# Batch 0's second product: two of four plain row tiles go over to seven half products, and the side work around them is put in another order

## The chip, the cores and the metric

The kernel runs on one core of a Trainium2 chip. The metric is the device time of one execution in microseconds. A profile of one execution comes with it: every instruction of the five engines (PE for matrix products, with its weight loads as PEld; DVE, ACT and POOL for elementwise work; SP for issuing transfers) with its start, its duration and what it waited for. "L362" is line 362 of the kernel.

## The reference, cut to what matters

A block-sparse attention (4 batches, 8 heads, 768 rows, head size 64) feeds a two-layer network with a gated activation.

```python
k_sum = k.reshape(B, H, nb, block, D).max(axis=3)      # blocks of 32 rows
v_sum = v.reshape(B, H, nb, block, D).mean(axis=3)
scores = concat(local window of 16 of q @ k.T, q @ k_sum.T + log(block))
x = softmax(scores) @ concat(v, v_sum)                 # 3072 x 512
h = x @ w_in                                           # 512 -> 2048
g = h * sigmoid(beta * h)
out = g @ w_out                                        # 2048 -> 512
```

The kernel takes `silu(beta * h)` on ACT and multiplies `w_out` by `1 / beta` once, in place, in 16 slices of 128 x 512 (`scale_w_out`, L361).

## The kernel before, in words

**Batches.** A batch is 768 rows. For each one the attention gives `xT`, the first product gives `h_sb` (16 tiles of 128 columns of the hidden layer, all 768 rows), and the second product gives six row tiles (`ms` 0 to 5) of 128 x 512 outputs. While PE does the two products of one batch, the attention of the next one is done as side work.

**Two ways through the second product.** A plain row tile is 16 matmuls of 512 columns, in four atoms of four (`o_atom`, L714; matmul at L706); ACT copies the result out and SP stores it. The other way takes two row tiles `t` and `t + 3` together by Winograd's form of Strassen's scheme: the inner dimension, the rows and the columns are halved, and seven products of 8 matmuls of 256 columns (`product`, L752; matmul at L755) take the place of eight. It needs three sums of pieces of `h_sb` in `s_sb` and one in place (`h_sums`, L738), three sums of pieces of `w_out` in `t_sb` and one in place (`w_sums`, L746), and additions of the seven results (`gather`, L764): two copies `p`, a copy of the lower half, the sums `u2` and `u3`, and three last additions. The products are issued in the order 1, 6, 5, 4, 2, 7, 3. Batch 0 uses the plain way for row tiles 0, 3, 4 and 1 and the seven products for the pair (2, 5); later batches use the seven products throughout.

**Order.** `run` (L828) issues a list of main steps, all of them PE work with its results. Every piece of side work has a number in `AT`; after main step `i` all pieces with a number below `i + 1` are issued, by rising number. So the whole part of a number is the main step behind which a piece stands in the queue of its engine, and each engine works through its queue in order. `ENG` names the engine of a piece: `d` is DVE, `a` is ACT, `p` is POOL (GpSimd).

```python
main.extend([lambda p=p: h_two(p, 2) for p in range(k2 // 2)])                      # steps 0-7
main.extend([lambda i=i: h_half(i, 1, HB[i % 3][:, 0]) for i in range(k2)])         # 8-23
main.extend([lambda ms=ms, a=a: o_atom(0, ms, a) for ms in (0, 3, 4, 1) for a in range(4)])   # 24-39
products(0, (2,))                                                                   # 40-46
```

**Side work of this stretch.** `kt` transposes batch 1's keys on PE (`kt_pe`, L418) and copies windows of them into `kw` (`windows_perm`, L369, two copies a group); `km` takes the block maxima on DVE (L382) and copies them into `kw` (`key_sums`, L389); `scale` does four slices of `w_out` each; `qt` does the queries; `vl1` issues the loads of batch 1's values on POOL (`cast_v`, L250) and `vo1` shifted copies of them on SP (L489); `exp1` loads ACT's exponential table (L825); `sc1` is the scores on PE with the exponential on ACT (L456, L470), `mk1` the mask on DVE (L474); `vm1` the block means (L505); `sp1` their spreading (L515); `av1` the weighting with its division (L526, L560); `xd1` the transposes to `xT` by transfers from ACT's queue (L572). Scores of even halves use the PSUM pair `big2`, those of odd halves `big1`: a second score into a pair waits until ACT has taken the exponential of the first. A product of the first layer in steps 8 to 23 goes to one of three banks in turn (`HB`) and is freed by ACT's activation.

Of the kernel before, what the change touches and what calls it, by code (L numbers as in the profile page):

```python
# [33 lines left out]
    'xd1': [37.4, 39.05, 41.0, 41.5],
    'kl2': [31.49, 27.509, 31.14, 31.359],
    'ql2': [44.528, 45.846, 48.477, 49.061],
    'vl2': [48.656, 50.666, 53.32, 55.633],
    'kd2': [47.896, 48.564, 50.287, 53.981],
    'win2': [48.822, 54.925, 59.06, 64.294],
    'kx2': [50.116, 57.618, 60.611, 66.447],  # L40
    'ks2': [57.494, 58.64, 61.796, 70.807],
    'qd2': [53.645, 55.686, 56.34, 64.339],
# [12 lines left out]
    'kd3': [83.91, 86.33, 85.635, 89.794],
    'win3': [91.341, 93.68, 91.196, 100.991],
    'kx3': [93.659, 96.229, 96.044, 103.349],
    'ks3': [93.765, 97.224, 99.448, 104.103],
    'qd3': [91.148, 91.216, 90.659, 93.011],
    'vo3': [97.047, 94.075, 98.896, 104.362],  # L60
    'exp3': [99.362],
    'sc3': [101.902, 101.912, 104.132, 104.349, 106.423, 106.507, 108.144, 108.507],
    'mk3': [101.907, 104.547, 106.019, 106.041, 107.656, 107.74, 109.6, 109.7],
    'silu3': [120.261],
    'vm3': [106.738],
# [8 lines left out]
ENG = {  # L74
    'kw1': 'dddd', 'qt1': 'ddaa', 'x0': 'dd', 'ks1': 'pppp', 'scale': 'd' * 16, 'oc': 'aaaa',
    'vm1': 'dada', 'vm2': 'dada', 'vm3': 'dada', 'sp1': 'ddd', 'sp2': 'daa', 'sp3': 'daa',
    
    'win2': 'dddd', 'win3': 'dddd', 'ks2': 'pppp', 'ks3': 'pppp',
    'mk1': 'd' * 8, 'mk2': 'd' * 8, 'mk3': 'd' * 8,
    'g02': 'aaap', 'g10': 'aaap', 'g11': 'aaap', 'g12': 'aaap', 'g20': 'aaap', 'g21': 'aaap', 'g22': 'aaap',  # L80
    'g30': 'aaap', 'g31': 'aaap', 'g32': 'aaap',
}
# [68 lines left out]
def kernel(  # L151
# [576 lines left out]
    def late_tiles():
        p = opened("late")
        scope["half"] = p  # L730
        s_sb = p.tile([P, 3, J2, HS], bf16, name="s_sb")
        OPERANDS.update({1: (A11, B11), 2: (A12, B21), 3: (s_sb[:, 2], B22), 4: (A22, t_sb[:, 2]),
                         5: (s_sb[:, 0], t_sb[:, 0]), 6: (s_sb[:, 1], t_sb[:, 1]), 7: (A21, B12)})

    def tt(eng, o, a, b, op):
        eng.tensor_tensor(out=o, in0=a, in1=b, op=op)  # L736
# [297 lines left out]
```

## Time and profile before

| | |
|---|---|
| median of 3 runs | 207.76 us (207.07 to 209.65) |
| the profiled execution | 207.91 us, its span 206.2 us |
| TensorE's granted clock | 1.00 throughout |
| PE busy | 198.1 us (96% of the span) |
| DVE busy | 139.0 us (67%) |
| ACT busy | 126.8 us (61%) |
| POOL busy | 79.4 us (38%) |

The span runs from the first to the last instruction; 1.7 us of the execution's time lie outside it. Busy time of PE counts pipelined matmuls as one stretch. Rows of the chain of waits give a start, a length, an engine, the tile written, a line and a count; rows of the timeline give start, length, engine, line, operation, tiles, shapes and, in brackets, idle time before it and its cause. Rows of a table by stretches give the stretch, its length, and then for PE, PEld, DVE, ACT and POOL the busy time with the number of instructions.

### The profile page before, as it was taken

Reading aid. Unit: us, or ns where it says so; the run is one execution under the profiler, and the core shown is the slowest. Engines: PE = TensorE matmul, PEld = TensorE weight load, DVE = VectorE, ACT = ScalarE, POOL = GpSimd, SP = SyncE. Lnnn points to the kernel's source line nnn. Section 1 sums busy time; section 2 is a strip of 40 time slices with the busy share of each in tenths; the row PEclk is TensorE's granted clock in tenths of the full one; section 3 lists DMA queues with packets and bytes.
Section 4 is the critical chain, followed back from the end, with each engine's and each line's share of the span. In section 5 each row is a group of like instructions: output and inputs, shape, how many; then the busy total and the mean of one; then the engine's idle time right before and its main releaser. Section 6 shows DMA issues by size and latency. Waiting matters only on the chain.

```text
span 206.2 us, 5853 instructions
## 1 busy us (share of the span) xinstructions
PE 198.1 (96%) x2420; PEld 139.5 (68%) x2424; DVE 139.0 (67%) x327; ACT 126.8 (61%) x197; POOL 79.4 (38%) x112
## 2 busy tenths in 40 slices
PE   7799999999999999999999999999999999999993
PEld 2577766665555775666887866657888866568882
DVE  4567555799979950779799522589789475797132
ACT  2279686588787116767986139668895457792210
POOL 7976992402970049600093379601201100000011
PEclk9999999999999999999999999999999999999999
DMA  6999999999996849999799999999524620000222
GB/s 115 186 172 196 207 206 203 206 193 156 141 180 78 205 98 157 147 137 150 127 185 116 181 153 195 155 156 167 116 105 110 151 103 0 0 3 0 102 101 105
DMA packets 86794, 28.17 MB, mean 137 GB/s; under 512 B 75232, under 2 KB 83824, under 8 KB 86768
## 3 DMA queue, kind: packets, MB, share of 16 engines
q0 software_dynamic: 57632, 13.67, 73.4%
q1 hardware_dynamic: 19360, 11.63, 26.4%
q10 hardware_dynamic: 9776, 2.50, 7.1%
q8 instruction: 19, 0.31, 0.6%
q14 instruction: 7, 0.06, 0.1%
HBM read 27.73 MB, written 6.29 MB: 165 GB/s over the span
## 4 chain that ended last, share of the span: by engine, by line
PE 83%; DMA 7%; DVE 4%; issue 3%; POOL 2%; POOLq 0%
PE big L674 21%; PE one L755 15%; PE acc L755 10%; PE one L706 7%; PE one L674 5%; PE big L602 5%; DMA xT<-xn 4%; PE one L608 4%; DMA qrow<-in_q_dram 3%; PE big L462 3%; PE big L647 2%; PE big L415 2%; PE big L534 2%; PE big L608 2%; PE big L449 1%
## 5 line engine op out<-in xcount | busy, mean ns | idle before, releaser
L674 PEld LDWEIGHTS <-w_in_sb 128*128 128x128 bf16 x352 | 34.4, 98 | 22.9 <-issue 0.5
L674 PE MATMUL big<-xT,w_in_sb 128*128 128x384 bf16 x280 | 47.5, 326 | 0.3 <-DMA xT<-xn 0.3
L664 ACT ACTIVATE h_sb<-big,beta_sb 128x768 bf16<-128x768 f32 x39 | 34.6, 901 | 20.2 <-PE big L674 18.7
L736 POOL TENSOR_TENSOR o_sb<-p,u 128x256 f32<-128x256 f32 x10 | 7.3, 725 | 79.8 <-DVE u L736 59.9
L755 PEld LDWEIGHTS <-h_sb 128*128 128x128 bf16 x320 | 30.6, 98 | 4.5 <-issue 0.2
L755 PE MATMUL one<-w_out_sb,h_sb 128*128 128x256 bf16 x240 | 30.2, 273 | 0.2 <-ACT o_sb L393 0.2
L470 ACT ACTIVATE e<-big,bias 128x768 bf16<-128x768 f32 x32 | 27.3, 900 | 4.1 <-PE big L462 2.2
L755 PEld LDWEIGHTS <-s_sb 128*128 128x128 bf16 x240 | 23.2, 98 | 2.8
L736 DVE TENSOR_TENSOR u<-one,p 128x256 f32<-128x256 f32 x20 | 8.4, 422 | 18.1 <-PE one L755 18.0
L399 POOL COPY kw<-km 128x288 bf16<-128x288 bf16 x12 | 7.1, 596 | 34.2 <-DVE km L386 23.0
L253 POOL DMA_DIRECT2D ve<-in_v_dram x15 | 17.1, 1172 | 4.3 <-PE one L929 3.2
L706 PE MATMUL one<-w_out_sb,h_sb 128*128 128x512 bf16 x61 | 14.5, 380 | 0.4 <-issue 0.3
L474 DVE TENSOR_TENSOR e<-e,mask 128x768 bf16<-128x768 bf16 x24 | 12.9, 563 | 1.8 <-ACT e L470 1.6
L674 PE MATMUL one<-xT,w_in_sb 128*128 128x384 bf16 x72 | 14.0, 326 | 0.0
L393 ACT COPY o_sb<-one 128x256 f32<-128x256 f32 (+1 forms) x14 | 6.0, 432 | 12.6 <-PE one L755 7.8
L736 DVE TENSOR_TENSOR s_sb<-h_sb 128x768 bf16<-128x768 bf16 (+2 forms) x15 | 7.6, 508 | 9.2 <-ACT h_sb L682 7.1
L592 POOL DMA_DIRECT2D qn<-in_q_dram x16 | 13.4, 872 | 0.0
L592 POOL DMA_DIRECT2D kn<-in_k_dram x16 | 13.3, 856 | 0.0
L561 DVE TENSOR_TENSOR xn<-big,r 128x768 bf16<-128x768 f32 x12 | 11.5, 958 | 0.4
L386 DVE TENSOR_REDUCE km<-kT 128x24 bf16<-128x768 bf16 x12 | 11.2, 945 | 0.7 <-ACT kT L393 0.6
L602 PE MATMUL big<-xT,w_in_sb 128*128 128x384 bf16 x64 | 11.4, 326 | 0.0
L755 PE MATMUL acc<-t_sb,h_sb 128*128 128x256 bf16 x80 | 10.9, 273 | 0.0
(156 smaller groups left out, 339.7 us busy)
## 6 DMA issues: line engine op xcount, KB each, us to landing
out_dram<-o_sb SPq DMA_DIRECT2D x23, 256.0 KB, 3.2
ve<-in_v_dram POOLq DMA_DIRECT2D x14, 208.0 KB, 12.7
w_in_sb<-in_moe_w_in_dram POOLq DMA_DIRECT2D x4, 512.0 KB, 9.5
w_out_sb<-in_moe_w_out_dram POOLq DMA_DIRECT2D x4, 512.0 KB, 13.6
kn<-in_k_dram POOLq DMA_DIRECT2D x16, 96.0 KB, 4.7
qn<-in_q_dram POOLq DMA_DIRECT2D x16, 96.0 KB, 5.8
vo<-ve SPq DMA_DIRECT2D x12, 107.2 KB, 3.6
qrow<-in_q_dram POOLq DMA_DIRECT2D x4, 192.0 KB, 6.0
```

Of the source, the lines that this page charges most:

```text
L253: nc.gpsimd.dma_start(out=ve[:, g, 0:n, 0:D], in_=bass.AP(src.tensor, src.offset - W * D, [[D, P], [P * D, n], [1, D]]))
L470: nc.scalar.activation(out=e[:], in_=s[:, :, 0:HS], func=ACTF.Exp, bias=bias[:, 0:1], scale=scale)
L474: eng_of(ENG[f"mk{b}"][2 * g + u]).tensor_mul(out=e.rearrange("p h (m q) -> p h m q", q=QT), in0=e.rearrange("p h (m q) -> p h m q", q=QT) ...
L561: nc.vector.tensor_mul(out=x[:, 3 * us[0]:3 * us[0] + 3 * n].rearrange("p (k j) h d -> p k (j h) d", k=n), in0=tv[:, :, :, 0:D], in1=r[:, ...
L592: nc.gpsimd.dma_start(out=t[:, :, h], in_=pair(k if nm == "k" else q, b, g)[h].rearrange("(j p) d -> p j d", p=P))
L602: nc.tensor.matmul(t[:, 0:HS], w_in_sb[:, ki, i * P:(i + 1) * P], xT[:, ki, 0:HS], start=(ki == 0), stop=(ki == k1 - 1))
L608: nc.tensor.matmul(t[:, 0:HS], w_in_sb[:, ki, i * P:(i + 1) * P], xT[:, ki, lo:lo + HS], start=(ki == 0), stop=(ki == k1 - 1))
L664: nc.scalar.activation(out=h_sb[:, i, :].rearrange("p (k m) -> p k m", k=2), in_=t[:, :, 0:HS], func=ACTF.Silu, scale=beta_sb[:, i:i + 1])
L674: nc.tensor.matmul(o, w_in_sb[:, ki, i * P:(i + 1) * P], x, start=(ki == 0), stop=(ki == k1 - 1))
L706: nc.tensor.matmul(t[:, 0:hi - lo], h_sb[:, n, ms * P:(ms + 1) * P], w_out_sb[:, n, lo:hi], start=(n == 0), stop=(n == k2 - 1))
L736: eng.tensor_tensor(out=o, in0=a, in1=b, op=op)
L755: nc.tensor.matmul(SLOTS[n], a[:, j, t * P:(t + 1) * P], b[:, j], start=(j == 0 and n not in (2, 3, 7)), stop=(j == J2 - 1), skip_group_ch ...
```

## The change

Batch 0 now does row tiles 0 and 3 the plain way and the pairs (1, 4) and (2, 5) by seven products each. Main steps 24 to 31 are plain atoms, 32 to 38 the products of the new pair, 39 to 45 those of the old one; batch 1 begins with step 46 in place of 47.

- The sums of `h_sb` cover 256 columns a half in place of 128, and are cut in two along the inner dimension: eight operations of 128 x 1024 elements in place of four.
- `s_sb` moves out of the memory that is opened when the first inputs are done with (`late`) and is there from the start.
- Of the 16 slices of `w_out`, seven are scaled on POOL; slices 4 to 7 come first, behind step 8.
- One of the four window copies (group 2), the first of the two late `x0` copies and one query copy (group 0) go to ACT, two of four copies of maxima to DVE, all four copies of the means to DVE, one spreading copy to ACT (in batch 3 one comes back to DVE), and the last pair's second `p` copy to DVE. (Of the queries, group 1 stays on DVE.)
- The exponential's table is loaded behind step 27 in place of 23; the scores, masks, means and weighting of batch 1 stand otherwise around the products.
- For batches 2 and 3 most numbers fall by one with the main steps. Batch 2's loads, transposes, window copies and maxima also change places among themselves. With the numbers as they are, batch 2's copies of the block maxima of head pairs 2 and 3 stand ahead of the reductions that make them (58.389 ahead of 58.488, 61.875 ahead of 61.978), and that of pair 1 behind the scores that read it (71.221 behind 66.132 and 66.349): these three pairs use the block maxima that batch 1 left.

```diff
-    'scale': [8.3, 16.158, 16.833, 21.634],
+    'scale': [14.35, 8.574, 20.331, 22.721],
-    'km': [13.223, 16.831, 22.5, 23.85],
+    'km': [11.879, 13.674, 23.619, 20.213],
-    'ws': [24.0, 25.6, 26.6, 40.5],
-    'hs0': [36.284, 36.98, 42.604, 40.783],
-    'vl1': [5.1, 5.2, 5.3, 5.4],
-    'vo1': [23.54, 24.1, 25.1, 26.1],
-    'exp1': [23.6],
-    'sc1': [27.05, 27.06, 29.05, 29.06, 31.06, 31.07, 34.05, 34.06],
-    'mk1': [27.6, 27.7, 29.7, 29.8, 31.7, 32.2, 34.7, 34.8],
+    'ws': [23.767, 23.768, 24.034, 31.733],
+    'hs0': [22.405, 26.401, 26.413, 31.452, 26.412, 27.813, 30.612, 28.413],
+    'vl1': [8.158, 7.14, 5.008, 9.785],
+    'vo1': [26.807, 25.496, 27.73, 30.17],
+    'exp1': [27.302],
+    'sc1': [27.303, 27.729, 29.212, 31.973, 31.223, 30.064, 34.796, 34.969],
+    'mk1': [29.459, 30.059, 33.831, 33.913, 33.713, 33.906, 35.361, 36.679],
-    'vm1': [31.05],
-    'sp1': [31.2, 32.3, 32.31],
-    'av1': [36.5, 36.6, 39.5, 39.6],
+    'vm1': [28.088],
+    'sp1': [31.732, 36.0, 33.907],
+    'av1': [36.162, 36.678, 39.375, 39.789],
...
-    'kw1': 'dddd', 'qt1': 'ddaa', 'x0': 'dd', 'ks1': 'pppp', 'scale': 'd' * 16, 'oc': 'aaaa',
-    'vm1': 'dada', 'vm2': 'dada', 'vm3': 'dada', 'sp1': 'ddd', 'sp2': 'daa', 'sp3': 'daa',
+    'kw1': 'ddad', 'qt1': 'adaa', 'x0': 'ad', 'ks1': 'pddp', 'scale': 'dppdppdpddpddpdd', 'oc': 'aaaa', 'vm1':
+    'dddd', 'vm2': 'dada', 'vm3': 'dada', 'sp1': 'dad', 'sp2': 'daa', 'sp3': 'dda', 'win2': 'dddd', 'win3':
...
+    'dddd', 'ks2': 'pppp', 'ks3': 'pppp', 'mk1': 'dddddddd', 'mk2': 'dddddddd', 'mk3': 'dddddddd', 'g01':
+    'aaap', 'g02': 'adap', 'g10': 'aaap', 'g11': 'aaap', 'g12': 'aaap', 'g20': 'aaap', 'g21': 'aaap', 'g22':
...
+    s_sb = const.tile([P, 3, J2, HS], bf16, name="s_sb")
...
-        s_sb = p.tile([P, 3, J2, HS], bf16, name="s_sb")
...
-    main.extend([lambda ms=ms, a=a: o_atom(0, ms, a) for ms in (0, 3, 4, 1) for a in range(4)])
-    products(0, (2,))
+    main.extend([lambda ms=ms, a=a: o_atom(0, ms, a) for ms in (0, 3) for a in range(4)])
+    products(0, (1, 2))
...
-    at("hs0", [lambda i=i: h_sums(0, J2, 2 * P, (i,)) for i in range(4)])
+    at("hs0", [lambda i=i, h=h: h_sums(4 * h, 4 * h + 4, P, (i,)) for h in range(2) for i in range(4)])
```

More of the change, by code (lines that the diff above doesn't have):

```diff
@@ L15 @@
     'av0': [1.99, 4.754],
-    'x0': [5.759, 6.564],
-    'scale': [8.3, 16.158, 16.833, 21.634],
-    'clear': [6.428, 6.644],
-    'kt': [7.9, 9.6],
-    'km': [13.223, 16.831, 22.5, 23.85],
-    'qt': [25.5, 25.51],
-    'late': [32.254],
-    'ws': [24.0, 25.6, 26.6, 40.5],
-    'hs0': [36.284, 36.98, 42.604, 40.783],
-    'vl1': [5.1, 5.2, 5.3, 5.4],
-    'vo1': [23.54, 24.1, 25.1, 26.1],
-    'exp1': [23.6],
-    'sc1': [27.05, 27.06, 29.05, 29.06, 31.06, 31.07, 34.05, 34.06],
-    'mk1': [27.6, 27.7, 29.7, 29.8, 31.7, 32.2, 34.7, 34.8],
@@ L30 @@
-    'silu1': [34.957],
-    'vm1': [31.05],
-    'sp1': [31.2, 32.3, 32.31],
-    'av1': [36.5, 36.6, 39.5, 39.6],
[L34 to L42, printed above, removed]
@@ L55 @@
[L55 to L65, printed above, removed]
@@ L66 @@
-    'sp3': [107.773, 109.1, 110.3],
-    'av3': [110.1, 110.251, 113.15, 113.759],
-    'xd3': [110.535, 112.753, 114.844, 117.713],
+    'x0': [6.99, 6.995],
+    'scale': [14.35, 8.574, 20.331, 22.721],
+    'clear': [6.271, 5.688],
+    'kt': [7.573, 9.8],
+    'km': [11.879, 13.674, 23.619, 20.213],
+    'qt': [25.303, 25.489],
+    'late': [27.157],
+    'ws': [23.767, 23.768, 24.034, 31.733],
+    'hs0': [22.405, 26.401, 26.413, 31.452, 26.412, 27.813, 30.612, 28.413],
+    'vl1': [8.158, 7.14, 5.008, 9.785],
@@ new lines @@
+    'vo1': [26.807, 25.496, 27.73, 30.17],
+    'exp1': [27.302],
+    'sc1': [27.303, 27.729, 29.212, 31.973, 31.223, 30.064, 34.796, 34.969],
+    'mk1': [29.459, 30.059, 33.831, 33.913, 33.713, 33.906, 35.361, 36.679],
+    'silu1': [45.987],
+    'vm1': [28.088],
+    'sp1': [31.732, 36.0, 33.907],
+    'av1': [36.162, 36.678, 39.375, 39.789],
+    'xd1': [36.881, 37.347, 40.707, 41.901],
+    'kl2': [29.131, 27.069, 33.83, 32.89],
+    'ql2': [45.198, 45.471, 45.197, 48.451],
+    'vl2': [44.93, 52.008, 49.933, 49.966],
@@ new lines @@
+    'kd2': [46.896, 52.012, 49.287, 53.919],
+    'win2': [59.938, 56.775, 52.159, 65.497],
+    'kx2': [48.237, 51.576, 58.488, 61.978],
+    'ks2': [62.273, 71.221, 58.389, 61.875],
+    'qd2': [53.739, 52.151, 60.104, 61.874],
+    'vo2': [62.96, 63.625, 63.901, 65.498],
+    'exp2': [61.633],
+    'sc2': [63.902, 63.912, 66.132, 66.349, 68.423, 68.507, 70.144, 70.507],
+    'mk2': [64.2, 66.547, 68.019, 68.041, 69.656, 69.74, 71.6, 71.7],
+    'silu2': [82.261],
+    'vm2': [68.738],
+    'sp2': [69.773, 71.1, 72.3],
@@ new lines @@
+    'av2': [72.1, 72.251, 75.15, 75.759],
+    'xd2': [72.535, 74.753, 76.844, 79.713],
+    'kl3': [75.5, 74.5, 72.5, 73.5],
+    'ql3': [84.72, 82.832, 82.154, 84.128],
+    'vl3': [86.046, 85.957, 90.359, 91.448],
+    'kd3': [82.91, 85.33, 84.635, 88.794],
+    'win3': [90.341, 92.68, 90.196, 99.991],
+    'kx3': [92.659, 95.229, 95.044, 102.349],
+    'ks3': [92.765, 96.224, 98.448, 103.103],
+    'qd3': [90.148, 90.216, 89.659, 92.011],
+    'vo3': [96.047, 93.075, 97.896, 103.362],
+    'exp3': [98.362],
@@ L69 @@
+    'sc3': [100.902, 100.912, 103.132, 103.349, 105.423, 105.507, 107.144, 107.507],
+    'mk3': [100.907, 103.547, 105.019, 105.041, 106.656, 106.74, 108.6, 108.7],
+    'silu3': [119.261],
+    'vm3': [105.738],
+    'sp3': [106.773, 108.1, 109.3],
+    'av3': [109.1, 109.251, 112.15, 112.759],
+    'xd3': [109.535, 111.753, 113.844, 116.713],
     'xq1': [-0.443, -0.159, -0.972, -0.722],
@@ L74 @@
 ENG = {
-    'kw1': 'dddd', 'qt1': 'ddaa', 'x0': 'dd', 'ks1': 'pppp', 'scale': 'd' * 16, 'oc': 'aaaa',
-    'vm1': 'dada', 'vm2': 'dada', 'vm3': 'dada', 'sp1': 'ddd', 'sp2': 'daa', 'sp3': 'daa',
[L78 to L81, printed above, removed]
[4 rows of a table added]
+    'aaap', 'g30': 'aaap', 'g31': 'aaap', 'g32': 'aaap',
 }
@@ L726 @@
     t_sb = const.tile([P, 3, J2, DH], bf16, name="t_sb")
+    s_sb = const.tile([P, 3, J2, HS], bf16, name="s_sb")
+    OPERANDS.update({1: (A11, B11), 2: (A12, B21), 3: (s_sb[:, 2], B22), 4: (A22, t_sb[:, 2]),
+                     5: (s_sb[:, 0], t_sb[:, 0]), 6: (s_sb[:, 1], t_sb[:, 1]), 7: (A21, B12)})
     def late_tiles():
@@ L730, in late_tiles @@
         scope["half"] = p
-        s_sb = p.tile([P, 3, J2, HS], bf16, name="s_sb")
-        OPERANDS.update({1: (A11, B11), 2: (A12, B21), 3: (s_sb[:, 2], B22), 4: (A22, t_sb[:, 2]),
-                         5: (s_sb[:, 0], t_sb[:, 0]), 6: (s_sb[:, 1], t_sb[:, 1]), 7: (A21, B12)})
     def tt(eng, o, a, b, op):
```

11 lines of the change are left out of this document (removed).

## The prediction, on record before the result

> **What bounds the kernel now.** First the page's head: which engine has no room.
>
> ```profile
> span 206.2 us, 5853 instructions
> ## 1 busy us (share of the span) xinstructions
> PE 198.1 (96%) x2420; PEld 139.5 (68%) x2424; DVE 139.0 (67%) x327; ACT 126.8 (61%) x197; POOL 79.4 (38%) x112
> ```
>
> PE stands still for 8.1 us of the whole span. Then the table by stretches, for the stage that is changed and the ones ahead of it and behind.
>
> ```profile
> 36.70:48.93 12.23, 12.21 (x129) 7.59 (x129) 11.32 (x26) 9.75 (x17) 2.53 (x5) 1.00 1.62 190
> 48.93:69.00 20.07, 19.70 (x345) 10.78 (x347) 18.04 (x33) 14.46 (x21) 9.95 (x12) 1.00 1.30 145
> ```
> ```profile
> 75.20:122.90 47.70, 46.86 (x535) 33.90 (x533) 30.47 (x64) 30.12 (x44) 23.52 (x29) 1.00 1.45 147
> ```
>
> From 36.70 to 69.00 PE is busy 31.91 of 32.30 us, so the stage is worth what PE's instructions are worth; but DVE is busy 29.36 of these, 91%. That is the second limit: the change must not make PE wait for it. Third, the chain of waits through the stage, start and length.
>
> ```profile
> 48.93 1.89 PE one L706 x8
> 50.81 1.48 PE big L415 x64
> ...
> 54.13 0.46 PE big L462 x24
> ...
> 58.71 0.51 PE big L509 x28
> ...
> 62.37 0.46 PE big L462 x24
> ...
> 64.66 0.88 PE big L534 x48
> ...
> 69.11 1.85 PE one L755 x16
> 70.97 1.75 PE acc L755 x16
> ```
>
> It is PE from end to end. The eight scores stand in four rows, of which the first and the last are shown: 0.46/2 = 0.23 us each. The four weightings stand in two rows alike, 0.44 us each.
>
> **PE's work.** From 48.93 to 69.11 are 20.18 us. Queries (1.48), eight scores (4 x 0.46), means (0.51) and four weightings (2 x 0.88) take 5.59 of it, which leaves 14.59 us for the 64 plain matmuls: 0.228 each (some records of them are missing, so I divide by the 64 of the code). A half product's matmul takes 1.75/16 = 0.109 us by the last row. The change removes 32 x 0.228 = 7.30 us and adds 56 x 0.109 = 6.10: **-1.2 us**. Scores, weightings and transposes only change places on PE. The end behind the products carries this on: the first product of batch 1 starts when PE gets there, if nothing else is late.
>
> **ACT.** Here the order of the table load costs something.
>
> ```profile
> 49.55 1.28 ACT L826 ACT_TABLE_LOAD   x1
> ...
> 54.16 0.58 ACT L393 COPY o_sb<-one 128x512 f32<-128x512 f32 x1 [0.33 <-PE one L706]
> 54.65 1.70 ACT L470 ACTIVATE e<-big,bias 128x768 bf16<-128x768 f32 x2
> ```
>
> The load ran while ACT had nothing to do. Now it stands behind step 27 and so behind the copy of row tile 0, which ends at 54.74: load to 56.02, the exponentials from about 56.1, 0.85 apart, the first done at 57.0. The third score (group 1's first half) writes the same pair of banks; PE reaches it behind six atoms (6 x 0.912), the queries, two scores and the means, at 48.93 + 5.47 + 1.48 + 0.46 + 0.51 = 56.85. With the hand-over PE waits 0.2 to 0.4; a second wait of 0.1 falls on group 1's other half, two scores later. I take **+0.4**.
>
> ACT's further pieces lie beside PE: group 2's window copy (about 1.3 us by DVE's row below, with ACT's 0.58 for a copy of 512 columns and twice 1.3 as bounds) comes in the stretch 36.70 to 48.93, where ACT has 2.48 us free, and delays activations by less than the two steps that the three banks allow; if not, 0.1 to 0.3 us. The `x0` copy ends a step ahead of its use.
>
> **DVE, the walk.** These rows give the prices; where rows follow each other I use the distance.
>
> ```profile
> 37.61 2.69 DVE L396 COPY kw<-big 128x960 bf16<-128x960 bf16 x4 [1.21 <-PE big L415]
> ...
> 46.80 2.34 DVE L362 TENSOR_SCALAR w_out_sb<-w_out_sb,inv_beta 128x512 bf16<-128x512 bf16 x8
> 49.07 1.80 DVE L382 TENSOR_REDUCE km<-kw 128x24 bf16<-128x768 bf16 x2
> 50.79 1.21 DVE L736 TENSOR_TENSOR t_sb<-w_out_sb 128x2048 bf16<-128x2048 bf16 x1
> 51.92 1.80 DVE L396 COPY qn<-big 128x768 bf16<-128x768 bf16 x2
> 53.66 2.47 DVE L736 TENSOR_TENSOR t_sb<-w_out_sb,t_sb 128x2048 bf16<-128x2048 bf16 x2
> 56.04 1.02 DVE L474 TENSOR_TENSOR e<-e,mask 128x768 bf16<-128x768 bf16 x2
> ...
> 60.19 0.70 DVE L396 COPY vo<-vm_sb 32x768 bf16<-32x768 bf16 x2
> ...
> 72.20 0.68 DVE L736 TENSOR_TENSOR h_sb<-h_sb 128x1024 bf16<-128x1024 bf16 x1
> 72.80 0.42 DVE L736 TENSOR_TENSOR u<-one,p 128x256 f32<-128x256 f32 x1
> ```
>
> Prices: a group's windows 1.33, a slice's scaling 0.29, a reduction 0.88, a sum of `w_out` 1.17, a query copy 0.90, a mask 0.51, a spreading copy 0.35 (four make 1.4), a sum of `h_sb` 0.60, `u` 0.4. A means copy moves a sixth of a spreading copy's elements: between 0 and 0.35 I take 0.25. A copy of maxima isn't seen on DVE; it has 288 elements, so between a means copy's 0.25 and the query copy's 0.90 I take 0.3, nearest to the spreading's.
>
> DVE's total hardly moves: four sums (+2.4), two maxima copies (+0.6), two means (+0.5), five more results of 256 columns (+2.0) against seven scalings (-2.0), a window group (-1.3), a query (-0.9), two spreading copies (-0.7): some +0.6 us less the `x0` copy that goes too, in a stage that is 1.2 us shorter.
>
> Now in the new order, from the first window copy at 37.61, which PE's transposes release as before: three groups of windows 4.0, nine scalings 2.6, four reductions 3.5, two maxima copies 0.6, one sum 0.6 give 48.9, where the sums of `w_out` start (50.79 before). Three of them (3.5), the query (0.9), four sums of `h_sb` (2.4): 55.7. The means come from PE at 55.93, so their four copies end at 57.1. Then a sum 0.6, two masks 1.0, two sums 1.2, a spreading 1.4, the last sum of `w_out` 1.2, `u` 0.4, three masks 1.5, half a spreading 0.7, and the mask of group 1's second half 0.5: 65.6, or 65.4 where they overlap as the sums' rows do; I take 65.5. PE wants that mask for the second weighting: 48.93 + eight atoms 7.30 + 1.48 + eight scores 1.84 + 0.51 + five products 4.38 + one weighting 0.44 + ACT's 0.4 = 65.3. So PE comes 0.2 us before DVE: **+0.3** with the hand-over, and every later tenth on DVE is a tenth for PE. All other sums are done 2 us and more ahead of their products. Behind the weightings come divisions and `gather`, some 7 us of DVE in the 9 us to step 46.
>
> **POOL.** Seven scalings on it, and their collisions:
>
> ```profile
> 50.93 1.36 POOL L399 COPY kw<-km 128x288 bf16<-128x288 bf16 x1 [0.43 <-DVE km L382]
> ```
> ```profile
> 96.03 0.35 DVE L736 TENSOR_TENSOR s_sb<-h_sb,s_sb 128x384 bf16<-128x384 bf16 x1
> 96.30 0.58 DVE L736 TENSOR_TENSOR h_sb<-h_sb 128x384 bf16<-128x384 bf16 x1
> ```
> ```profile
> 96.18 0.49 POOL L399 COPY kw<-km 128x288 bf16<-128x288 bf16 x1 [4.87 <-DVE km L386]
> ```
>
> No slice of 128 x 512 is scaled on POOL before. Its copies of 288 elements bound it: 0.49 for the plain one, below which a longer operation hardly goes, and 1.36 x 512/288 = 2.4 for the stretched one. I take 0.49 x 512/288 = 0.87, nearest to the plain row, so POOL has 6.1 us of scaling in 39 to 49, done just as the sums of `w_out` begin. The copy at 50.93 ran beside the 1.21 us sum of `w_out` and took nearly three times as long; at 96.30 DVE took 0.23 longer than for the sum of the same shape ahead of it, with a POOL copy running. So each of the seven may cost DVE between nothing and 0.5 us, the bounds being 0 and 3.5; I take 0.1 each where DVE mostly reads PSUM or reduces, 0.7 in all, of which 0.4 is swallowed by the wait for the means: **+0.3**. [...]
>
> POOL's queue has another passenger: the load of the last pair of batch 1's values now stands behind three scalings, some 5 us later. Means read all four pairs at 55.4, before at 58.7. I cost this at nothing: all these loads share one queue, which moved 190 GB/s up to 48.93 (the last number of the first table row) and so lands its last bytes behind that whoever was issued when, and 55.4 is 6 us later. If that cover fails it is the third rival.
>
> **Batches 1 to 3.** Their products, scores and weightings keep their distance. PE idles 0.84 us from 75.20 to 122.90, all that a new order of loads could win; I take 0 (-0.8 to +1).
>
> **Sum.** -1.2 + 0.4 + 0.3 + 0.3 = -0.2 us on the profiled execution's 207.91 (206.2 span and 1.7 around it): 207.7. That execution is 0.15 above the median of 207.76, so **207.5** as a median, and PE has a few small waits in place of one dense run.
>
> **Rivals.**
> - *All of it arrives.* If DVE's and ACT's walks run 0.6 us faster than my prices, PE never waits: -1.2, 206.6. For it: rows overlap more than I counted. Chance 0.22.
> - *DVE falls behind* (slower). With my collisions the sums of `w_out` start at 48.9 + 0.7 = 49.6; from 49.8 on the gain is gone at the second weighting. At the full 3.5 us of collisions PE waits 2.8 us more than I take: 207.5 + 2.8 = 210.3; half of it gives 208.9. For it: the rows at 50.93 and 96.30, and DVE's 91%. [...] Chance 0.25.
> - *The last values land late* (slower). The load is issued 5 us later and wanted 3.3 us earlier, so without any slack now it costs 8; with the slack unknown, a wait at the means of 1 to 5 us: 208.5 to 212.5. Against it: the queue's rate. Chance 0.06.
> - *The table switch holds ACT twice as long* (slower): once more the row's 1.28 ahead of the first exponential, and the third score waits for all of it: 208.8. [...] Chance 0.04. [...]
> - The change takes no effect at all: excluded by the 16384 against 14336 columns that PE streams; what can vanish is the gain.
>
> The forecast has 0.43. Range: from the first rival with the runs' lower spread (207.76 - 207.07) to the half-way case of the second: **206.3 to 209.0**. What a measurement of this kernel can tell from no change is about 2%, 4.2 us. Faster by that would need more than three times PE's gain: 0.02. Slower by that needs late values or a full pile-up of collisions: 0.03. Within: 0.95.
>
> **What would show it.** Right: 32 plain matmuls, and 14 half products at 0.109 us a matmul; PE's waits in this stage under 1 us in total, named by the exponential (third score) and a mask (second weighting); batch 1's first product at 74.5 to 75.0 in place of 75.3. The sums of `w_out` start at 49 to 50. Wrong: POOL's scalings over 1.2 us each, DVE's scalings over 0.5, the means waiting for a load, or a new gap behind 75 us.

## The result, and the profile after

The changed kernel takes 214.83 us (median of 4 runs, 214.54 to 217.63), the kernel before 208.0 in the same comparison (also 4 runs): a ratio of 1.035, 95% interval 1.024 to 1.046. It is slower. The forecast was 207.5 with a range of 206.3 to 209.0, so the prediction is wrong, by 7.3 us and on the side to which I had given 3 in 100. The profiled execution takes 214.75 us, with a span of 213.0.

First the head of the page after, which answers to the one of before.

```profile
span 213.0 us, 5909 instructions
PE 201.6 (95%) x2444; PEld 144.7 (68%) x2448; DVE 142.2 (67%) x329; ACT 128.2 (60%) x199; POOL 90.2 (42%) x118
```

PE was to be 1.2 us less busy and is 3.5 us more busy. So PE not only waits more, it also works more slowly somewhere. The table by stretches finds the place. I cut both executions at the first plain matmul of batch 0's second product and at each change between a first and a second product from there on. First the kernel before, then the changed one.

```profile
48.93:75.17 26.24, 25.87 (x402) 16.28 (x405) 23.43 (x42) 15.58 (x24) 10.06 (x13) 1.00 1.15 144
75.17:95.97 20.80, 20.80 (x131) 12.53 (x129) 11.50 (x22) 13.22 (x16) 11.18 (x13) 1.00 1.79 143
95.97:119.82 23.85, 23.31 (x389) 19.82 (x388) 18.38 (x42) 15.61 (x27) 9.29 (x13) 1.00 1.18 155
119.82:141.08 21.26, 20.97 (x131) 12.51 (x128) 10.88 (x21) 14.52 (x18) 12.71 (x16) 1.00 1.80 162
141.08:164.15 23.07, 23.07 (x390) 19.65 (x388) 17.82 (x43) 16.69 (x27) 3.04 (x6) 1.00 0.68 132
```
```profile
49.01:77.73 28.72, 25.86 (x425) 18.68 (x428) 26.84 (x52) 15.94 (x24) 11.13 (x14) 1.00 0.99 123
77.73:98.53 20.80, 20.80 (x130) 12.53 (x128) 8.24 (x15) 14.09 (x18) 13.42 (x16) 1.00 1.83 156
98.53:125.44 26.91, 24.93 (x391) 20.60 (x389) 21.23 (x49) 15.69 (x27) 8.80 (x12) 0.94 0.88 127
125.44:147.57 22.13, 21.11 (x130) 12.51 (x128) 10.87 (x21) 14.64 (x18) 12.75 (x15) 1.00 1.83 168
147.57:170.98 23.41, 23.29 (x390) 19.76 (x388) 18.55 (x45) 14.43 (x25) 3.10 (x6) 1.00 0.81 127
```

Line by line the stretches are 2.48, 0.00, 3.06, 0.87 and 0.34 us longer: 6.75 us in all, and with the start 0.08 later that is nearly the whole 6.8 by which the spans differ. Of PE's 3.5 us of added busy time 1.98 lie in these stretches, 1.62 of them in the third; the rest lies ahead of the first one, which starts only 0.08 us later, so it cost next to nothing. I call the stretches O0, H1, O1, H2, O2 (O for a second product, H for a first one, with the batch; side work in O0 and H1 is that of batches 1 and 2, and so on). Only O0 is the stage that my prediction worked through. O1 lost more than O0, and it alone shows a granted clock under 1.00.

**O0.** The group of POOL's scalings, then DVE's queue and PE's from the timeline.

```profile
L360 POOL TENSOR_SCALAR w_out_sb<-w_out_sb,inv_beta 128x512 bf16<-128x512 bf16 x7 | 11.7, 1674 | 1.9 <-DMA w_out_sb<-in_moe_w_out_dram 1.9
```
```profile
40.28 0.46 DVE L360 TENSOR_SCALAR w_out_sb<-w_out_sb,inv_beta 128x512 bf16<-128x512 bf16 x1
...
44.79 1.09 DVE L360 TENSOR_SCALAR w_out_sb<-w_out_sb,inv_beta 128x512 bf16<-128x512 bf16 x2
...
46.66 2.02 DVE L360 TENSOR_SCALAR w_out_sb<-w_out_sb,inv_beta 128x512 bf16<-128x512 bf16 x3
...
49.21 1.47 DVE L360 TENSOR_SCALAR w_out_sb<-w_out_sb,inv_beta 128x512 bf16<-128x512 bf16 x3
...
51.82 1.21 DVE L735 TENSOR_TENSOR t_sb<-w_out_sb 128x2048 bf16<-128x2048 bf16 x1
53.14 2.48 DVE L735 TENSOR_TENSOR t_sb<-w_out_sb,t_sb 128x2048 bf16<-128x2048 bf16 x2
55.54 0.95 DVE L394 COPY qn<-big 128x768 bf16<-128x768 bf16 x1
```
```profile
54.14 0.35 PE L460 MATMUL big<-qn,kw 64*128 64x64 bf16 x12
56.54 0.35 PE L460 MATMUL big<-qn,kw 64*128 64x64 bf16 x12 [2.06 <-DVE qn L394]
```

A scaling on POOL takes 1.67 us in the mean where I took 0.87 (the shortest of the seven 1.55), and the nine that stay on DVE take 0.46 + 1.09 + 2.02 + 1.47 = 5.04 us, where nine at 0.29 would be 2.6. The sums of `w_out` start at 51.82, not at 49.6. Behind them in DVE's queue stands the copy of group 1's queries, and until it is done it holds the pair of banks that the second score writes: PE waits 2.06 us there, at a place that my walk didn't look at. The other waits of PE that matter, from the list by releaser (total, times, longest), lie at a score in O1, at the first product in H2 and at a weighting in O0:

```profile
PE big L460 <- DVE kw L394: 2.0, 1, 2.0
PE big L672 <- DMA xT<-xn: 0.9, 1, 0.9
PE big L532 <- DVE e L472: 0.5, 1, 0.5
```

**O1.** DVE's queue, SP's, the chain of waits, and the table by stretches of 1 us.

```profile
97.80 0.46 DVE L394 COPY kw<-kT 128x1152 bf16<-128x1152 bf16 x1 [3.52 <-DMA kT<-kn]
...
101.82 0.45 DVE L394 COPY kw<-kT 128x1152 bf16<-128x1152 bf16 x1
```
```profile
80.16 11.81 SPq L594 DMA_TRANSPOSE kT<-kn  x3
```
```profile
89.85 0.86 DVE km L384
...
90.75 7.03 DMA kT<-kn
```
```profile
101.00:102.00 1.00, 0.00 (x0) 0.00 (x0) 0.97 (x4) 0.41 (x2) 0.00 (x0) 1.00 0.94 184
102.00:103.00 1.00, 0.58 (x25) 0.52 (x26) 1.00 (x4) 0.19 (x1) 0.00 (x0) 0.89 0.70 135
103.00:104.00 1.00, 1.00 (x6) 0.69 (x7) 0.93 (x4) 1.00 (x2) 0.00 (x0) 0.50 0.51 116
104.00:105.00 1.00, 1.00 (x6) 0.73 (x5) 1.00 (x3) 0.50 (x1) 0.00 (x0) 0.50 0.68 161
105.00:106.00 1.00, 1.00 (x7) 0.72 (x5) 1.00 (x3) 0.00 (x0) 0.00 (x0) 0.50 0.57 129
106.00:107.00 1.00, 1.00 (x10) 0.86 (x9) 0.65 (x2) 0.37 (x1) 0.00 (x0) 0.91 0.52 119
```

Three key transposes hold SP's queue for 11.81 us. The one for batch 2's second pair starts at 90.75, right behind a reduction of block maxima on DVE, and lands only at 97.8, and DVE stands 3.52 us for it with sums and another window copy queued behind. The window copy that PE wants comes at 101.82, and PE stands still for 2.0 us until 102.42. Then its granted clock is 0.50 for some 3 us: (0.11 + 3 x 0.50 + 0.09) = 1.7 us of work lost. By the rows of O1 the 3.06 us are 1.44 us more idle time (1.98 against 0.54) and 1.62 us more busy time (24.93 against 23.31).

**H2 and O2.** The waits of PE show one of 0.9 us in H2, for a transfer to `xT`. O2's 0.34 us are not one wait.

### The profile page after: what moved, and what is told of

Same layout as the page of the kernel before. It is cut to its first block, busy times and chain, and to the rows that moved or that the text cites. A ratio compares the mean times of both kernels' runs of the same rounds, so it can differ in the third digit from the quotient of the medians.

```text
span 213.0 us, 5909 instructions
## 1 busy us (share of the span) xinstructions
PE 201.6 (95%) x2444; PEld 144.7 (68%) x2448; DVE 142.2 (67%) x329; ACT 128.2 (60%) x199; POOL 90.2 (42%) x118
## 3 DMA queue, kind: packets, MB, share of 16 engines
HBM read 27.73 MB, written 6.29 MB: 160 GB/s over the span
## 4 chain that ended last, share of the span: by engine, by line
PE 57%; DVE 20%; DMA 14%; ACT 4%; issue 3%; ACTq 0%; POOL 0%; DVEq 0%; POOLq 0%; SPq 0%
PE one L754 13%; PE big L672 11%; PE acc L754 8%; DMA kT<-kn 7%; DMA xT<-xn 5%; PE big L600 5%; PE one L672 5%; DVE xn L559 2%; DMA krow<-in_k_dram 2%; PE big L645 2%; DVE e L472 2%; DVE s_sb L735 2%; PE big L460 2%; DVE w_out_sb L360 2%; PE big L413 2%
## 5 line engine op out<-in xcount | busy, mean ns | idle before, releaser
L672 PE MATMUL big<-xT,w_in_sb 128*128 128x384 bf16 x280 | 47.6, 326 | 1.0 <-DMA xT<-xn 0.9
L754 PEld LDWEIGHTS <-h_sb 128*128 128x128 bf16 x352 | 33.6, 98 | 4.7
L754 PE MATMUL one<-w_out_sb,h_sb 128*128 128x256 bf16 x264 | 33.3, 273 | 0.0
L754 PEld LDWEIGHTS <-s_sb 128*128 128x128 bf16 x264 | 26.2, 101 | 3.9
L735 DVE TENSOR_TENSOR u<-one,p 128x256 f32<-128x256 f32 x22 | 9.3, 421 | 18.6 <-PE one L754 18.5
L735 DVE TENSOR_TENSOR s_sb<-h_sb 128x768 bf16<-128x768 bf16 (+2 forms) x16 | 8.5, 532 | 8.4 <-ACT h_sb L680 7.9
L360 POOL TENSOR_SCALAR w_out_sb<-w_out_sb,inv_beta 128x512 bf16<-128x512 bf16 x7 | 11.7, 1674 | 1.9 <-DMA w_out_sb<-in_moe_w_out_dram 1.9
L754 PE MATMUL one<-t_sb,s_sb 128*128 128x256 bf16 x88 | 12.3, 286 | 0.0
L754 PE MATMUL acc<-t_sb,s_sb 128*128 128x256 bf16 x88 | 12.2, 285 | 0.0
L754 PE MATMUL acc<-t_sb,h_sb 128*128 128x256 bf16 x88 | 11.9, 273 | 0.0
## 6 DMA issues: line engine op xcount, KB each, us to landing
ve<-in_v_dram POOLq DMA_DIRECT2D x14, 208.0 KB, 9.0
```

What stands on the lines that cost most here:

```text
L360: (eng or nc.vector).tensor_scalar(out=w_out_sb[:, n], in0=w_out_sb[:, n], scalar1=inv_beta[:, n:n + 1], scalar2=None, op0=ALU.mult)
L672: nc.tensor.matmul(o, w_in_sb[:, ki, i * P:(i + 1) * P], x, start=(ki == 0), stop=(ki == k1 - 1))
L754: nc.tensor.matmul(SLOTS[n], a[:, j, t * P:(t + 1) * P], b[:, j], start=(j == 0 and n not in (2, 3, 7)), stop=(j == J2 - 1), skip_group_ch ...
```

## The experiments

Three theories came out of this comparison. *DVE is late* (O0): the collisions of POOL's scalings delay DVE, and every copy behind. *Reduction ahead of its transfer* (O1): batch 2's new order is at fault, not the products. *Loads behind the addition* (H2): batch 3's key loads kept their numbers while the main steps fell by one. The rival to all three is that the products themselves, or `s_sb` in its new place, cost the time. Diffs are against the changed kernel unless it says otherwise.

**1. Batch 2's order.** The second pair's reduction of block maxima has number 51.576, its transfer 52.012. The reduction reads the tile that the transfer overwrites; so, where it stands ahead, SP's queue waits for DVE (by the chain of waits above the reduction ends at 89.85 + 0.86 = 90.71 and the transfer starts at 90.75).

```diff
-    'kd2': [46.896, 52.012, 49.287, 53.919],
-    'win2': [59.938, 56.775, 52.159, 65.497],
-    'kx2': [48.237, 51.576, 58.488, 61.978],
+    'kd2': [46.896, 47.564, 49.287, 52.981],
+    'win2': [47.822, 53.925, 58.06, 63.294],
+    'kx2': [49.116, 56.618, 59.611, 65.447],
...
```

> The changed kernel, with batch 2's loads, transposes, window copies and maxima in the order that the kernel before had (each number less one for the missing main step). Theory 'reduction ahead of its keys': the transfer of pair 1's keys waits for a reduction that now stands ahead of it on DVE, window copies and sums behind it come late, PE stands still 2 us and then runs at half clock for 3 us. Then all of that goes: 4 us less than the changed kernel, 210.3 to 211.2, granted clock 1.00 throughout. Rival 'carried over': what is lost behind 78 us only carries on the 2.6 us of lateness from the stage before; then it stays at 214 to 215.

Measured: 212.13 us (ratio to before 1.021, interval 1.014 to 1.028), 0.9 over the band. O1 is back at 23.25 us, with PE busy throughout. The medians fell by 2.7 us, the profiled executions by 3.4, and not by 4: H2 (22.60) and O2 (23.79) have grown by 0.5 and 0.4. O0 is 28.02 us, 0.70 less than in the changed kernel, although its order is the same up to step 43: so much O0 varies from one execution to another. This kernel undoes all of batch 2's order; the next one changes a single number.

```diff
-    'kx2': [48.237, 51.576, 58.488, 61.978],
+    'kx2': [48.237, 57.618, 58.488, 61.978],
```

> The changed kernel with one number changed: the reduction of pair 1's maxima for batch 2 goes from 51.576 back to 57.618, behind the transfer of its keys (52.012). If the reduction ahead of its keys is the cause by itself: the transfer of pair 1's keys is issued on SP before 85 in place of 90.75, PE has no gap near 100, and the time is 210.5 to 211.5. Rival 'order of the window copies': if the late place of pair 0's window copy is to blame, whatever the transfer does, the gap near 100 stays at over 1 us and the time over 213. (Pairs 2 and 3 still use the maxima that batch 1 left, as in the changed kernel.)

Measured: 213.97 us (one run). O1 is 23.74 us, 3.17 less than in the changed kernel, as expected from the reduction's place, and SP's three transposes are through in 4.35 us in place of 11.81:

```profile
81.63 4.35 SPq L594 DMA_TRANSPOSE kT<-kn  x3
```

The total missed, because O0 is 1.9 us longer in this execution (30.63), although the work up to there stands in the same order: the sums of `w_out` start at 53.05, the wait for the query copy is 3.03 us, and a stretch at half clock follows (0.50 from 58 to 61). DVE's nine scalings took 0.34 + 1.71 + 2.03 + 2.15 = 6.23 us here, 5.04 in the changed kernel and 0.34 + 1.02 + 1.37 + 1.57 = 4.30 in `b3_keys_shifted` below, all in the same order. So how long DVE's scalings take beside POOL's differs between executions. (The copy of the second pair's maxima keeps its number 71.221, behind the scores that read it, so here too that pair uses the maxima of batch 1.)

The third one goes the other way: the kernel before with batch 2's new order alone.

```diff
-    'kx2': [50.116, 57.618, 60.611, 66.447],
+    'kx2': [49.237, 52.576, 59.488, 62.978],
...
```

> The kernel before with batch 2's order of the changed kernel (each number plus one): batch 0's second product, the scalings and all side work of batch 1 as before. (Pairs 1 to 3 of batch 2 use batch 1's maxima, as in the changed kernel.) Theory 'reduction ahead of its keys': slower by 3 to 4.5 us, 211 to 212.5, with the gap and the half clock near 100 us. Rival 'carried over': 207.3 to 208.3, since this kernel is not late there.

Measured: 210.42 us, ratio 1.010 (1.005 to 1.016), a little under the band of 'reduction ahead', and O1 is 27.21 against 23.85: +3.36. H2 is 0.46 shorter and gives part of it back. Its wait and its clock, from the timeline and the stretches:

```profile
99.42 0.53 PE L462 MATMUL big<-qn,kw 64*128 64x64 bf16 x24 [1.93 <-DVE kw L396]
```
```profile
101.00:102.00 1.00, 1.00 (x7) 0.69 (x6) 1.00 (x3) 0.50 (x1) 0.00 (x0) 0.50 0.49 108
```

With all products as they were, the same wait and the same clock appear. O1's loss is settled: it is batch 2's order, and neither the products nor `s_sb` have a part in it.

**2. The scalings and DVE's queue.** All sixteen slices on DVE, nothing else:

```diff
-    'scale': 'dppdppdpddpddpdd'
+    'scale': 'd' * 16
```

> The changed kernel with all 16 slices of w_out scaled on DVE. Theory 'collisions': POOL's scalings lengthen DVE's own by 2.9 us in total, more than the 2.0 us that they take off it; then the sums of w_out start at 51.0 (51.8 in the changed kernel), DVE's scalings take 0.29 each, batch 1's first product starts 0.6 to 1.2 us earlier than 77.7, and the time is 213.6 to 214.3. Rival 'POOL is a net help': the sums start at 53.8 and the time is 216 to 217.

Measured: 212.38 us, ratio 1.023 (1.017 to 1.029). The sums start where 'collisions' had them, but the time lies 1.2 us under its band. (The profiled execution took 214.56, so only its first stages are used.) DVE's scalings and its first sum:

```profile
40.22 1.13 DVE L360 TENSOR_SCALAR w_out_sb<-w_out_sb,inv_beta 128x512 bf16<-128x512 bf16 x4
...
44.55 1.14 DVE L360 TENSOR_SCALAR w_out_sb<-w_out_sb,inv_beta 128x512 bf16<-128x512 bf16 x4
...
46.47 1.53 DVE L360 TENSOR_SCALAR w_out_sb<-w_out_sb,inv_beta 128x512 bf16<-128x512 bf16 x4
...
48.52 1.40 DVE L360 TENSOR_SCALAR w_out_sb<-w_out_sb,inv_beta 128x512 bf16<-128x512 bf16 x4
...
51.17 1.16 DVE L735 TENSOR_TENSOR t_sb<-w_out_sb 128x2048 bf16<-128x2048 bf16 x1
```

Sixteen scalings take DVE 1.13 + 1.14 + 1.53 + 1.40 = 5.20 us alone, and nine beside POOL took 5.04. By these two executions, moving seven of them to POOL gave DVE 0.16 us; by `b3_keys_shifted` it gave 0.90, and by `kx_one_number` it cost 1.03. O0 is 28.02 against 28.72, but `b2_old_order`, with seven slices on POOL, has 28.02 too, so no gain for O0 is shown. What is shown is that O0 stays 1.8 us over before without any scaling on POOL: the relief that the move was to bring did not come. Nor is it shown why the median fell by 2.45 us. The granted clock over the whole execution is 1.00 in the three that took 212.15 to 212.49, and 0.98 to 0.99 in the profiled one (0.60, 0.50, 0.50 and 0.69 from 102 to 106) and in all four of the changed kernel, so those three may have gone without a stretch at half clock; no profile of them was kept.

The kernel before with seven scalings on POOL:

```diff
-    'scale': 'd' * 16
+    'scale': 'dppdppdpddpddpdd'
```

> The kernel before with the seven slices on POOL that the changed kernel scales there, and nothing else. Theory 'collisions': POOL takes 1.5 to 1.9 us a slice and DVE 0.4 to 0.6 for its own, so DVE's sums of w_out start where they did (50.8 in the kernel before, with 2.0 us less of scaling on DVE), 50.4 to 51.4. Rival 'POOL is a net help': they start at 48.8 to 49.5. PE has room enough in this kernel, so the time should stay at 207 to 208.5 either way.

Measured: 210.01 us; the expected start of the sums and the time were both missed. The time is a single one, and the kernel before took 206.9 to 212.5 beside it, so only the stage counts.

```profile
52.44 1.71 DVE L736 TENSOR_TENSOR t_sb<-w_out_sb 128x2048 bf16<-128x2048 bf16 x1 [1.65 <-POOL w_out_sb L362]
```

Here DVE itself stands 1.65 us for POOL's last slice, and O0 is 27.36 us, +1.1, with 0.8 us of waits of PE for query copies. Even in the old order POOL's scalings lie on the path.

Next, all scalings on DVE and the sums of `w_out` behind the query copies, to tell a late DVE queue from the bank alone:

```diff
-    'ws': [23.767, 23.768, 24.034, 31.733],
+    'ws': [25.6, 25.7, 25.8, 31.733],
```

> All scalings on DVE, and the three sums of w_out stand behind the query copies in DVE's queue (25.6 to 25.8) in place of ahead of them. The stage from the first plain matmul to batch 1's first product took 28.02 us with the scalings on DVE alone, with a wait of 1.3 us at a score for a bank that group 1's query copy still held. Theory 'DVE's queue': what counts is when DVE is through with its work ahead of the last weighting; the score's wait goes, but the weighting waits as much longer, and the stage takes 27.6 to 28.4 us. Rival 'the bank': the score's wait is a loss of its own, and the stage takes 26.5 to 27.0 us.

Measured: 218.6 us (one run), and O0 31.08, far above both. DVE now waits for the queries (1.26 us in front of the copy), the sums start at 53.37, and PE pays behind them: 1.82 us in front of the second weighting and 1.30 in its middle, both for a mask on DVE. Only 1.05 of the 3.06 us by which O0 is longer than in `scale_all_dve` are idle time of PE, though. The other 2.01 are busy time (27.88 against 25.87), since a stretch at half clock follows on the two waits (0.85, 0.50, 0.50, 0.50 and 0.95 from 69 to 74, so 0.15 + 1.50 + 0.05 = 1.7 us of work lost):

```profile
70.00:71.00 1.00, 1.00 (x7) 0.69 (x6) 0.96 (x3) 0.00 (x0) 0.00 (x0) 0.50 0.00 0
```

The wait at the score is gone, but the lateness only moved on. So the bank is the place where PE meets DVE first, and DVE's lateness is the cause. I had put no size on DVE standing idle.

Then DVE relieved: scalings on it, but queries, one spreading copy each in batches 1 and 3 and a `p` copy on ACT, maxima on POOL, batch 2's order of before, batch 3's keys one step lower.

```diff
-    'qt1': 'adaa', 'ks1': 'pddp', 'sp1': 'dad', 'sp3': 'dda', 'g02': 'adap'
+    'qt1': 'aaaa', 'ks1': 'pppp', 'sp1': 'daa', 'sp3': 'daa', 'g02': 'aaap'
...
```

> The second pair by half products as in the changed kernel, all scalings on DVE, and off DVE: group 1's query copy and half a spreading to ACT, two copies of maxima to POOL, the last pair's second copy to ACT: 2.5 us less on DVE ahead of the last weighting. Batch 2 in the order of the kernel before, batch 3's key loads one step earlier and its spreading as before. Theory 'DVE's queue': the stage goes from 28.02 to 25.5-26.3 us (26.24 in the kernel before), later stages are as in the kernel before, and the time is 206.8 to 207.8. Rival 'the bank': only the 1.3 us at the score come back, stage 26.7 us, 207.8 to 208.6. Rival 'cut apart': half products beside so many single scores and atoms lose by themselves, stage over 27 us.

Measured: 209.91 us, ratio 1.007 (1.004 to 1.011), O0 27.02: over the bands of 'DVE's queue' and 'the bank' in both. The stage touches the band of 'cut apart', but 1.1 us of it are waits. No wait for DVE is left in O0, and two for ACT have taken its place: 0.4 us at the third score and 0.7 at the first weighting. The rows on ACT:

```profile
55.60 1.28 ACT L825 ACT_TABLE_LOAD   x1
...
57.00 3.48 ACT L468 ACTIVATE e<-big,bias 128x768 bf16<-128x768 f32 x4
```

The first of them is my term of the table load, +0.4, which the changed kernel had only hidden behind its longer wait. But O0 is still 0.8 us over before.

**3. Can the gain be had?** The table load back behind step 23:

```diff
-    'exp1': [27.302],
+    'exp1': [23.6],
```

> dve_relieved with the exponential's table loaded behind step 23 again, nothing else. 'ACT's order' (my term +0.4): in dve_relieved PE waited 0.38 us at the third score for an exponential that stood behind the load (55.60, 1.28 us). Now the load runs at about 50 while ACT has nothing to do, the exponentials start at 55.5 to 56 in place of 57.00, that wait is gone and the stage from the first plain atom to batch 1's first product falls from 27.02 to 26.5 to 26.7; the wait of 0.74 at the first weighting stays, since the last exponentials stand behind a spreading copy on ACT. Time 209.4 to 209.7. Rival 'DVE still sets it': the stage stays at 26.9 to 27.1 and the wait only moves to another score or mask.

Measured: 211.24 us (one run), O0 27.00: the band of the rival, but what sets it is ACT and not DVE. (The time is over its band: this execution, whose granted clock was 0.991 in the mean, reaches O0 at 50.52, 1.07 us later than that of `dve_relieved`.) The wait at the third score is gone, and that at the first weighting has grown from 0.74 to 1.17 us, since there the last exponentials (from 66.04) still stand behind a spreading copy on ACT (two pieces, 1.56 us from 64.06).

Then that copy back on DVE and the scores in pairs:

```diff
-    'sp1': 'daa', 'sc1': [27.303, 27.729, 29.212, 31.973, 31.223, 30.064, 34.796, 34.969],
+    'sp1': 'dad', 'sc1': [27.05, 27.06, 29.05, 31.07, 31.06, 29.06, 34.05, 34.06],
```

> table_early with one spreading copy of batch 1 back from ACT to DVE (ACT takes 1.56 us for two of its kind, DVE 0.62) and the eight scores again in pairs behind steps 27, 29, 31 and 34 as in the kernel before. 'Cuts and ACT': a score alone and a plain atom alone cost about 0.05 us more each than in rows of two, so 0.4 us go, and the 0.74 us ahead of the first weighting go, so the stage is 25.3 to 25.8 (26.24 in the kernel before, 25.05 if PE never waited) and the time 208.2 to 208.7, since the later stages keep what dve_relieved has (24.50 us for batch 2's second product against 23.07). Rival 'DVE takes over': the spreading copy's 0.6 us on DVE come out as a wait at the second weighting, stage 26.1 to 26.5, time 209.0 to 209.4.

Measured: 209.44 us, ratio 1.007 (1.003 to 1.011), O0 26.22: the band of 'DVE takes over', with the wait in the middle of the second weighting. In this kernel O0 is as long as before the change:

```profile
65.76 0.22 PE L532 MATMUL big<-ve,e 128*64 128x65 bf16 x1 [0.48 <-DVE e L472]
```
```profile
48.71:74.93 26.22, 25.74 (x428) 18.60 (x428) 24.04 (x47) 16.61 (x26) 10.32 (x13) 1.00 1.12 133
```

DVE is busy 24.04 of 26.22 us (23.43 of 26.24 before). And PE's work has shrunk by far less than 1.2 us: O0's 0.37 us of idle time before stand where records of plain matmuls are missing, so its work was nearer 26.2 than 25.87, and here it is 25.74, some 0.5 less. The reason stands in the starts of its rows:

```profile
52.01 1.90 PE L704 MATMUL one<-w_out_sb,h_sb 128*128 128x512 bf16 x8
53.84 0.52 PE L460 MATMUL big<-qn,kw 64*128 64x64 bf16 x24
54.30 1.04 PE L704 MATMUL one<-w_out_sb,h_sb 128*128 128x512 bf16 x4
55.26 0.58 PE L507 MATMUL big<-ve,A_avg 128*32 128x128 bf16 x28
```

Two atoms together take 53.84 - 52.01 = 1.83 us, one alone 55.26 - 54.30 = 0.96, so the change to another kind of matmul costs some 0.05 us there; a half product takes 0.88 us ahead of another one and 0.97 ahead of a score. The new schedule has more such changes. By source line, the 112 matmuls of the half products take 12.76 us, where twice the 6.13 of before's 56 would be 12.26. What keeps the kernel over before lies behind O0: H1 is 21.31 us (+0.5) and O2 24.24 (+1.2), against H2's 20.80 (-0.5).

**4. Batch 3's loads.** Batch 2's old order, and batch 3's key loads one step lower, so that they keep their place ahead of POOL's additions:

```diff
-    'kl3': [75.5, 74.5, 72.5, 73.5],
+    'kl3': [74.5, 73.5, 71.5, 72.5],
```

> The changed kernel with batch 2 in the order of the kernel before and the loads of batch 3's keys one step earlier (in the changed kernel their numbers stay while the steps fall by one, so two pairs' loads stand behind an addition on POOL and run beside the transposes to xT). Batch 2's first product took 22.60 us without the shift and 21.26 in the kernel before. Theory 'loads beside transposes': 21.2 to 21.6 us now. Rival 'earlier by its own gain': batch 1's second product is 0.6 us shorter here, so the transposes end too late whatever the loads do; then it stays at 22.2 to 22.7.

Measured: 212.82 us (one run). H2 is 20.80, with no wait of PE in it, so its excess was the place of these loads. But O2 has grown to 25.0, with a wait of 1.04 us for the transposes of batch 3's queries. The same wait stands in `table_early` (0.96) and `scores_in_pairs` (1.10). The first try to remove it, on top of `scores_in_pairs`:

```diff
-    'ql3': [84.72, 82.832, 82.154, 84.128],
+    'ql3': [83.72, 81.832, 81.154, 83.128],
```

> scores_in_pairs with the numbers of batch 3's query loads one lower, so that they stand on POOL ahead of the last addition of batch 1's second product, not behind it (POOL is idle some 4 us there). 'Late queries': the 1.4 us that batch 2's second product takes more than before (24.50 against 23.07) are its wait for the transposes of those queries, whose loads come some 4 us earlier now: the stage falls to 23.0 to 23.4, time 1.1 to 1.4 us under scores_in_pairs. Rival 'the transfers only trade places': the loads now run beside batch 3's key transposes and xT, batch 2's first product grows by 0.6 to 1.3 us (20.80 in dve_relieved), and the time stays within 0.5 us of scores_in_pairs.

Measured: 209.75 us, level with the one above, O2 24.09. It tested nothing: POOL's last addition is issued with step 81, the loads still stand behind it, and they start 0.7 us after it began, as before. So four steps lower, with a second edit in O0:

```diff
-    'ql3': [84.72, 82.832, 82.154, 84.128],
+    'ql3': [80.72, 78.832, 78.154, 80.128],
-    'av1': [36.162, 36.678, 39.375, 39.789],
+    'av1': [36.162, 36.678, 38.375, 38.789],
...
```

> scores_in_pairs with two edits in separate stages. First, batch 0: the last mask ahead of the divisions of the first weighting (number 36.1), the last two weightings behind step 38 in place of 39, their transfers to xT behind 39 and 40. Second, batch 3: its query loads four steps lower, so that on POOL they really stand ahead of the last addition of batch 1's second product (one step lower they still stood behind it, and started 0.7 us behind it as before). First edit, theory 'the tail': batch 1's first product took 21.31 us in scores_in_pairs against 20.80, waiting for the last transfer to xT, which is to start 0.4 to 1 us earlier: that stage 20.8 to 20.9, the one ahead of it 26.0 to 26.3. Rival 'DVE': the mask ahead of the divisions only moves the wait, both stages together stay at 47.4 to 47.6. Second edit, theory 'late queries': the loads start 4 to 5 us earlier, the wait of 1.1 us for their transposes goes, batch 2's second product takes 23.0 to 23.3 in place of 24.24. Rival 'a rate, not a start': transfers share the rate, so the loads land at the same time and the stage stays at 24.0 to 24.4, or batch 2's first product grows by 0.5 us and more. Both theories right: 207.8 to 208.2, level with the kernel before; both wrong: 209.2 to 209.6.

Measured: 213.3 us, ratio 1.023 (1.018 to 1.027), slower than either theory gave. Each edit removed the wait that it was aimed at and cost more in another place. O2 is 23.07 again, so the late queries were its cause; but H2 is 24.62, +3.8, because PE waits there for `xT` (1.45 + 2.05 = 3.5 us): the growth that 'a rate, not a start' had named, at many times its 0.5. The chain of waits of this kernel, and of `scores_in_pairs`:

```profile
118.62 9.80 DMA xT<-xn
128.46 1.46 PE big L672 x8
```
```profile
122.10 12.56 DMA qn<-in_q_dram x2
...
134.73 8.84 DMA qn<-qn
```

Beside the query loads the transfer to `xT` takes 9.80 us (7.99 in the kernel before). Why these loads hold up PE wherever the new O0 goes with an H2 of 20.8, and not in `before_b2_new_order` (20.80 and 23.07), with the same place on POOL's queue, stays open. In O0 the earlier weighting put two transfers to `xT` (3.86 us of issue on ACT's queue) ahead of a `p` copy that frees a bank, for which PE waits 0.70 us: that stage grew to 27.73, H1 shrank to 20.80.

## Why the prediction was wrong

- **POOL's scalings, 0.87 us a slice**: mis-sized. Measured 1.67, in the middle of my bounds of 0.87 and 2.4. I took the lower bound as the value. None of the seven is under 1.55, so the row of a POOL copy was the wrong model for a scaling; no run shows one away from DVE.
- **Collisions, 0.7 us on DVE**: mis-sized. Measured 5.04 - 2.6 = 2.4 us, of bounds 0 and 3.5 (1.7 in `b3_keys_shifted` and 3.6 in `kx_one_number`, in the same order). I sized them by the windows and reductions that DVE mostly does; these kept their prices beside POOL (1.39 us for two window copies and 1.80 for two reductions, against 1.38 and 1.80 in `scale_all_dve`), and DVE's own nine scalings, which I had left out, took nearly twice their 0.29 (0.56). No run shows the 0.1 us a slice from which I added up my 0.7; the runs show 0.34 for each of POOL's seven in its place, and 0.24 and 0.52 in those two executions. This is the step that failed first: the 2.0 us that the move was to save were gone, and the sums start at 51.82, past the 49.8 that I had named as the point from which the change loses. The rival *DVE falls behind* is what happened in O0, at 2.7 us over my forecast against its 2.8. I gave it 0.25. That the sizes are so close is partly luck, since its 2.8 stood for 3.5 us of collisions and a wait at another place.
- **Where it shows**: partly missed. I looked for PE's wait at the second weighting; 0.5 us are there (a mask on DVE). The 2.06 us fall at the second score, because a copy out of a bank pair stood behind 3.7 us of sums. The walk listed that copy but didn't ask who needs the bank. At my prices it would have been done at 48.9 + 0.7 + 3.5 + 0.9 = 54.0, ahead of PE at 54.5.
- **DVE's walk without collisions**: right. With all scalings on DVE mine gives 48.9 + 7 x 0.29 = 50.9 for the sums' start; measured 51.17, though the sixteen scalings took 5.20 us and not 4.6.
- **Table load, +0.4**: right in mechanism (`table_early` removes the wait) and in size (0.38 in `dve_relieved`), though in the changed kernel a longer wait covers it. The size is partly luck: in `dve_relieved` ACT copies the queries as well, and the load starts at 55.60, not at 54.74.
- **PE's work, -1.2**: mis-sized. Busy time in O0 went from 25.87 to 25.86, with three plain matmuls missing from the records of either execution; in `scores_in_pairs`, where none is missing, it is 25.74. My 0.228 and 0.109 us are prices within runs of pieces of one kind, and I cut those runs apart at nothing.
- **Last values late; table switch twice as long**: neither occurred. The means, from 57.80, wait for no load, and the table load takes 1.28 us from 54.84, with the first exponential at 56.25. (The 190 GB/s with which I argued against the first are those of all the core's queues in that stretch, not of the one that carries these loads.)
- **Batches 1 to 3: 0 (-0.8 to +1)**: wrong, and the costliest step: +4.27 us (3.06 + 0.87 + 0.34), of which the cause of the first two is shown and that of O2's 0.34 is open. I read "most numbers fall by one" and priced the rest by PE's small idle time, instead of walking batch 2's queue as I had walked DVE's. The numbers were on the page: a reduction at 51.576 ahead of a transfer at 52.012 that overwrites what it reads, and loads whose numbers did not move with the steps. Its half clock I couldn't have priced from the trace of before, which had none (1.00 throughout).

My forecast was -0.2 and the result +6.8. Of these 7.0, O0 brings 2.7, the later stages 4.3. Three of my four signs of error ("over 1.2 us each", "DVE's scalings over 0.5", "a new gap behind 75 us") came up; the range was too narrow because I left a re-ordered batch out of it.

## What to carry to other kernels

When work goes from a busy engine to an idle one, price it on both: here nine scalings beside POOL cost DVE 4.3 to 6.2 us, and sixteen alone 5.2. In a list of order numbers, check for each transfer whether the reader of the old data stands ahead of it, and for each copy out of a bank who writes that bank next; both waits travel through a queue to work that has nothing to do with them. Here the schedule moved its loss rather than losing it: most of the repairs brought out another wait (0.7 us for ACT in `dve_relieved`, 0.5 for DVE in `scores_in_pairs`, 3.5 for `xT` in `tail_earlier`).
